# Dense products behind attention values issued as four 128x32 column tiles, with values directly after a score visit

## The chip, the cores and the metric

One NeuronCore of one Trainium2 chip runs the whole program. The metric is the device time of one execution in microseconds, a median over runs. "Span" is the profile's length of one execution; here it is 1.7 to 1.9 us shorter than the time. All runs told here are of the state that the records call fast, so fast runs are compared with fast runs throughout. (A fast run can still hold a few microseconds at a lower granted clock, as the kernel before does with 0.71 from 65 to 70 us; where one does, the text says so.) In these profiles every matmul has its weight load (10,928 of each in the kernel before); these two instructions per matmul are meant wherever "rows" are counted.

## The reference, cut to what matters

```python
def _A_ref(x, wqkv, wo):                 # S = 2048, D = 512, 32 heads of 16, window 256
    q, k, v = ...                        # x @ wqkv
    scores = einsum(q, k) * Dh ** -0.5   # masked to the last 256 positions
    o = einsum(softmax(scores), v)
    return o @ wo
def _B_ref(x, w_gate, w_up, w_down):     # F = 1792
    return (sigmoid(x @ w_gate) * (x @ w_up)) @ w_down
x = x + A(layernorm(x)); x = x + B(layernorm(x))      # twice
```

## The kernel before

The program is laid out by a scheduler written in Python. It keeps assumed times for every engine and transfer, and emits instructions in the order that its plan gives. What it assumes is never waited for by time: semaphores guard every access, so a wrong assumption costs waits, not results. TensorE's stream has three forms. Scores use four row tiles (32 rows by 128 columns), values four column tiles (128 by 32), and all dense products (q, k, v, output, gate, up, down) use the whole array. The scheduler fills the time between two score "visits" with dense products.

```python
def product_steps(...):                      # one of the dense kinds, cut
    return [(mm_ns(w), lambda kt=kt, o=o: nc.tensor.matmul(
        self.banks[bank][:, o:o + w], lhsT=self.wq[:, kt, ...], rhs=self.xnT[key][0][:, kt, o:o + w], ...))
        for o in range(0, TGW, w) for kt in range(KT)]

def values(...):                             # 16 groups of four and more, cut
    for k, (where, Va, p) in enumerate(parts):
        for g, h in enumerate(heads):        # four heads, four column tiles
            nc.tensor.matmul(o, lhsT=Va[:, c0:c0 + 32], rhs=p(h), ..., tile_position=(0, 32 * g))

def pick(self):                              # what TensorE does next, cut
    if pv and (wait <= 600 or wait > 1e8 or held):
        return self.do_values(pv, spare)     # values shortly before the next visit
    ...
    pl.count(1)
    end = pl.matmul("d", ns)                 # 96 ns are added in the plan where the form changes
```

The softmax here doesn't subtract the row's maximum and nothing guards it: scores larger than these inputs give would overflow.

## Time and profile before

| | kernel before |
|---|---|
| time, median of 3 | 556.89 us |
| span | 555.0 us |
| TensorE busy, share of span | 543.1 us, 98% |
| TensorE rows (2 x 10,928 in the profile; the prediction counts 21,858) | 21,856 |
| changes of form on TensorE | 380 |

A busy share hides what lies between two matmuls, because the recorded durations overlap: a values matmul of 64 columns is recorded with 193 ns in the mean, while the next group of four starts 0.03 us later. What sets the pace is the distance between starts, so the argument works with starts.

The busy times by stretch show where the kernel is fed worst. Columns are busy us and instructions per engine, then granted TensorE clock, DMA share and GB/s:

```profile
0.00:100.00 100.00, 93.75 (x1923) 65.69 (x1923) 74.39 (x181) 74.91 (x78) 20.19 (x53) 0.97 0.52 133
100.00:480.00 380.00, 378.64 (x8480) 244.15 (x8480) 299.41 (x641) 307.82 (x340) 43.51 (x88) 1.00 0.33 57
```

From 100 to 480 us TensorE, the first engine in the row, misses 1.4 us of 380. The list of what TensorE waited for (waiter, what ended the wait: us in total, times, longest) is short:

```profile
PE bank L529 <- DVE xn L517: 2.3, 2, 1.8
PE bank L929 <- issue: 1.9, 1, 1.9
PE bank L1104 <- POOL ident L438: 1.4, 1, 1.4
```

The first and last are the start of the program. The one in the middle, "issue", waited for nothing that the profile knows.

### The profile page before, as it was taken

The numbers are of one execution on the slowest core, as the hardware profiler recorded it, in microseconds if no ns is written. First come the engines' busy times: TensorE is split into PE (matmuls) and PEld (weight loads), VectorE is DVE, ScalarE is ACT, GpSimd is POOL, SyncE is SP. The second block draws the span as 40 slices with busy tenths as digits, with TensorE's granted clock in tenths as the row PEclk, the third lists the DMA queues.
The fourth block names the chain that finished last, engine by engine and source line by source line (L and its number), as shares of the span: only waits on it lengthen the run. The fifth ranks groups of instructions, "written<-read, shape, count | busy, mean of one in ns | idle before, by whom it ended". The sixth has DMA issues, their size and how long they took to land.

```text
span 555.0 us, 24233 instructions
## 1 busy us (share of the span) xinstructions
PE 543.1 (98%) x10928; PEld 361.3 (65%) x10928; DVE 406.4 (73%) x893; ACT 402.3 (72%) x468; POOL 65.3 (12%) x145
## 2 busy tenths in 40 slices
PE   7999899999999999999999999999999999999996
PEld 6567666665766656765566666566667666767873
DVE  5769787898976798688887778877777756464432
ACT  2869688888988878778788788787788876422321
POOL 5202111222010120002020010200010000010000
PEclk8999899999999999999999999999999999999999
DMA  8991203352323352424361303621133412310000
GB/s 276 290 216 33 41 18 67 46 85 44 70 34 47 59 90 47 64 43 79 50 95 29 58 12 69 89 51 41 31 70 80 68 32 51 69 48 11 11 20 28
DMA packets 99191, 36.94 MB, mean 67 GB/s; under 512 B 81424, under 2 KB 99088, under 8 KB 99088
## 3 DMA queue, kind: packets, MB, share of 16 engines
q1 hardware_dynamic: 97216, 33.56, 30.8%
q8 instruction: 85, 1.39, 1.1%
q10 hardware_dynamic: 1872, 1.84, 1.1%
q14 instruction: 18, 0.15, 0.1%
HBM read 9.70 MB, written 2.10 MB: 21 GB/s over the span
## 4 chain that ended last, share of the span: by engine, by line
PE 90%; DVE 5%; issue 1%; ACT 1%; POOL 1%; DMA 1%; SPq 0%; ACTq 0%; DVEq 0%
PE bank L659 34%; PE bank L692 18%; PE bank L929 8%; PE Sps L850 7%; PE bank L569 5%; PE bank L598 5%; PE bank L634 5%; PE bank L720 5%; PE Sps L860 2%; PE bank L1104 2%; DVE st L495 1%; DMA xnT<-xn 1%; DVE xn L517 1%; POOL st L501 1%; DVE PTring L788 0%
## 5 line engine op out<-in xcount | busy, mean ns | idle before, releaser
L902 ACT ACTIVATE PTring<-Sps 128x2048 bf16<-128x2048 f32 (+1 forms) x122 | 225.9, 1852 | 28.2 <-PE Sps L850 27.0
L659 PE MATMUL bank<-xnT,wg 128*128 128x256 bf16 (+1 forms) x1008 | 139.0, 262 | 0.8 <-ACT OTs L550 0.5
L659 PE MATMUL bank<-xnT,wu 128*128 128x256 bf16 (+1 forms) x1008 | 139.8, 262 | 0.0
L671 ACT ACTIVATE th<-bank 128x256 bf16<-128x256 f32 x224 | 80.3, 388 | 62.1 <-PE bank L659 59.1
L674 DVE SCALAR_TENSOR_TENSOR hT<-th,bank 128x256 bf16<-128x256 bf16 x224 | 87.2, 414 | 47.2 <-ACT th L671 46.6
L692 PE MATMUL bank<-wd,hT 128*128 128x512 bf16 x448 | 114.3, 381 | 0.0
L659 PEld LDWEIGHTS <-wg 128*128 128x128 bf16 x1008 | 88.4, 98 | 28.5 <-issue 3.6
L659 PEld LDWEIGHTS <-wu 128*128 128x128 bf16 x1008 | 90.0, 98 | 13.7 <-issue 1.6
L500 POOL TENSOR_SCALAR st<-st 128x1 f32<-128x1 f32 x64 | 20.6, 321 | 422.9 <-DVE st L496 422.9
L788 DVE TENSOR_TENSOR PTring<-PTring,mask 128x1024 bf16<-128x1024 bf16 x64 | 43.9, 686 | 31.0 <-ACT PTring L902 30.8
L902 ACT ACTIVATE edge<-Sps 128x2048 bf16<-128x2048 f32 (+1 forms) x32 | 56.7, 1771 | 12.9 <-PE Sps L860 12.9
L692 PEld LDWEIGHTS <-hT 128*128 128x128 bf16 x448 | 41.4, 98 | 37.4 <-issue 1.6
L929 PEld LDWEIGHTS <-Vaug 128*32 128x32 bf16 x2880 | 44.1, 97 | 15.0 <-issue 13.0
L929 PE MATMUL bank<-PTring,Vaug 128*32 128x64 bf16 (+1 forms) x2880 | 52.0, 203 | 1.9 <-issue 1.9
L850 PE MATMUL Sps<-qT,kTp 32*128 32x64 bf16 (+3 forms) x1856 | 48.5, 219 | 0.5 <-DVE st L495 0.2
L550 ACT CAST OTs<-bank 128x512 bf16<-128x512 f32 x40 | 29.4, 736 | 24.4 <-PE bank L929 23.7
L929 PE MATMUL bank<-edge,Vl 128*32 128x64 bf16 x1024 | 44.7, 193 | 0.0
L495 DVE BATCH_NORM_STATS2 st<-xsb 128x6 f32<-128x512 bf16 x64 | 43.7, 683 | 0.2
L850 PEld LDWEIGHTS <-kTp 32*128 32x128 bf16 x1856 | 24.9, 93 | 28.2 <-issue 24.5
L501 POOL TENSOR_TENSOR st<-st,nhalf 128x1 f32<-128x1 f32 x64 | 40.9, 640 | 5.3
L788 DVE TENSOR_TENSOR edge<-edge,maske 128x1024 bf16<-128x1024 bf16 x60 | 40.3, 679 | 0.8 <-ACT edge L902 0.7
L929 PE MATMUL bank<-edge,Vh 128*32 128x64 bf16 x896 | 40.7, 193 | 0.0
(71 smaller groups left out, 554.9 us busy)
## 6 DMA issues: line engine op xcount, KB each, us to landing
Vl<-Vaug SPq DMA_DIRECT2D x32, 68.0 KB, 2.9
out_dram<-xsb SPq DMA_DIRECT2D x32, 64.0 KB, 1.9
Vh<-Vaug SPq DMA_DIRECT2D x28, 68.0 KB, 2.2
wg<-in_B_w_gate_dram SPq DMA_DIRECT2D x2, 896.0 KB, 7.9
wu<-in_B_w_up_dram SPq DMA_DIRECT2D x2, 896.0 KB, 10.9
wd<-in_B_w_down_dram SPq DMA_DIRECT2D x7, 256.0 KB, 5.1
wq<-in_A_wqkv_dram ACTq DMA_DIRECT2D x3, 512.0 KB, 7.3
xsb<-in_A_x_dram SPq DMA_DIRECT2D x6, 256.0 KB, 6.2
```

The lines of the kernel that those rows point to most:

```text
L495: nc.vector.bn_stats(out=st[:, 0:6], in_=self.xsb[:, t, :])
L501: nc.gpsimd.tensor_tensor(out=st[:, 8:9], in0=st[:, 9:10], in1=self.nhalf[:], op=ALU.pow)
L550: self.nc.scalar.copy(out=out, in_=in_)
L569: return [(mm_ns(w), lambda kt=kt, o=o: nc.tensor.matmul(self.banks[bank][:, o:o + w], lhsT=self.wq[:, kt, cq * P:cq * P + P], rhs=self.xn ...
L659: return [(mm_ns(w), lambda i=i, j=j, fc=fc, wt=wt, kt=kt: nc.tensor.matmul(pt[:, i, j, :], lhsT=wt[:, kt, fc * P:(fc + 1) * P], rhs=self. ...
L671: nc.scalar.activation(out=box["th"][0][:], in_=pt[:, 0, :], func=AF.Tanh, scale=0.5)
L674: nc.vector.scalar_tensor_tensor(out=self.hT[:, chunk, :], in0=box["th"][0][:], scalar=1.0, in1=pt[:, 1, :], op0=ALU.add, op1=ALU.mult)
L692: nc.tensor.matmul(self.banks[bank][:], lhsT=self.hT[:, c, o:o + P], rhs=self.wd[:, fc, :], start=fc == 0, stop=fc == FC - 1)
L788: done = pl.task({"DVE": dve_bf_ns(1024)}, lambda e: nc.vector.tensor_tensor(out=r, in0=r, in1=m.to_broadcast([P, 16, HP]), op=ALU.mult), ...
L850: nc.tensor.matmul(self.sps[:, m, o:o + n * HP], lhsT=kTp[32 * m:32 * m + 32, i, tt, e, :], rhs=self.qT[32 * m:32 * m + 32, i, q0:q0 + n * ...
L902: nc.scalar.activation(out=out, in_=src, func=AF.Exp, scale=scale)
L929: nc.tensor.matmul(o, lhsT=Va[:, c0:c0 + 32], rhs=p(h), start=k == 0 or t == 0, stop=k == len(parts) - 1 or t == 0, tile_position=(0, 32 * g))
```

## The change

The intent is to save changes of form. Behind a values call TensorE is already in the 128x32 form, so dense products are issued in that form too, until the next score visit. Values are moved right behind a visit, which puts two needed changes (dense to scores, scores to values) where there were four. Around this core, priorities, weight loads (seven pieces instead of two), startup and the assumed DMA times were retuned.

```diff
+    def in_tiles(self):
+        return self.pl.mode == "pv" and self.slot < len(self.visits)
+    def product(self, out, lhsT, rhs, start, stop):
+        if not self.in_tiles():
+            self.nc.tensor.matmul(out, lhsT=lhsT, rhs=rhs, start=start, stop=stop)
+            return
+        for g in range(4):
+            h = slice(32 * g, 32 * g + 32)
+            self.nc.tensor.matmul(out[h], lhsT=lhsT[:, h], rhs=rhs, start=start, stop=stop, tile_position=(0, 32 * g))
 ...  (all dense nc.tensor.matmul calls become self.product)
-        if pv and (wait <= 600 or wait > 1e8 or held):
+        if pv and (pl.mode != "d" or wait <= -1 or wait > 1e8 or held):
-        pl.count(1)
-        end = pl.matmul("d", ns)
+        tiles = self.in_tiles() and u.name[0] != "tp"
+        pl.count(4 if tiles else 1)
+        end = pl.matmul("pv" if tiles else "d", ns + 0 if tiles else ns)
 ...  (retuning, the part that matters below)
-DMA_LATENCY = 1500
+DMA_LATENCY = 1200
-            self.dma_free = max(self.dma_free, self.now + ns) + nbytes / 250.0
+            self.dma_free = max(self.dma_free, self.now + ns) + nbytes / 290.0
-        b = pl.dma(1800, 262144, turn, ...)
+        b = pl.dma(1240, 160000, turn, ...)
-        d = pl.dma(1190, 131072, turn2, ...)
+        d = pl.dma(1190, 20000, turn2, ...)
-            d = pl.dma(1190, P * D * 2, ...)           # the third transpose
+            d = pl.dma(1210, 20000, ...)
 ...  (priorities, loads in seven pieces, startup: cut)
```

More of the change, by code (lines that the diff above doesn't have):

```diff
@@ L389, in load_x, with load @@
             return done
-        def load(dst, src, nbytes, after=0, deps=(), prio=2, queue="SP"):
+        def load(dst, src, nbytes, after=0, deps=(), prio=4, queue="SP"):
             ns = max(520, 40 + nbytes / 1024 * 0.95)
@@ L399, in loads @@
             h = slice("qkv".index(k) * D, ("qkv".index(k) + 1) * D)
-            self.has_wq[k] = load(self.wq[:, :, h], wq_src[:, :, h], D * D * 2, prio=0, queue="ACT" if i < 3 else "SP")
+            self.has_wq[k] = load(self.wq[:, :, h], wq_src[:, :, h], D * D * 2, prio=0, queue="ACT" if i < 2 else "SP")
         def x_group(g, after):
             h = slice(g * NBG, (g + 1) * NBG)
-            ev = load_x(self.xsb[:, h, :], h, NBG, 2 if g > 1 else 2, after=after)
+            ev = load_x(self.xsb[:, h, :], h, NBG, 4 if g > 1 else 2, after=after)
             for t in range(g * NBG, (g + 1) * NBG):
@@ L411, in loads @@
         at += gap * 2
-        n = F // 2
+        n = F // 7
         gu = []
-        for i in range(2):
+        for i in range(7):
             h = slice(i * n, (i + 1) * n)
@@ L418, in loads @@
                 pair.append(load(w[:, :, h], src[:, :, h], D * n * 2, after=at))
-                at += gap * 7 // 2
+                at += gap * 7 // 7
             gu.append(pair)
@@ L423, in loads @@
                 at += gap * 2
-        self.has_gu = [gu[fc * 2 // FC] for fc in range(FC)]
+        self.has_gu = [gu[fc * 7 // FC] for fc in range(FC)]
         self.has_wd = Event()
@@ L455, in constants @@
         self.pl.free["POOL"] = 4000.0
+        self.pl.free["SP"] = self.pl.free["ACT"] = 750.0
+        self.pl.at(750.0)
+        self.pl.at(1500.0)
         self.pl.free["DVE"] = 3200.0
@@ L524, in layer_norm @@
         o = (t % NBG) * P
-        if key == ("p", 0, 0) or key[0] == "g" and self.by_pe(key[1], t):
+        if key[:2] == ("p", 0) and t < 4 or key[0] == "g" and self.by_pe(key[1], t):
             def steps(bank):
@@ L534, in evac @@
                 d = pl.task({"ACT": act_ns(KT * P), "DVE": dve_ns(KT * P) + 100}, lambda e: self.copy(
-                    e, self.xnT[key][0][:, :, o:o + P], pt), [u.done], 0)
+                    e, self.xnT[key][0][:, :, o:o + P], pt), [u.done], 0 if t < NBG else 4)
                 d.done.then(lambda: (self.give(box["xn"]), done.fire()))
@@ L540, in layer_norm @@
         else:
-            d = pl.dma(1190, P * D * 2, lambda: nc.sync.dma_start_transpose(
+            d = pl.dma(1210, 20000, lambda: nc.sync.dma_start_transpose(
                 out=self.xnT[key][0][:, :, o:o + P], in_=box["xn"][0][:]), [c.done], prio)
@@ L568, in steps @@
         def steps(bank):
-            return [(mm_ns(w), lambda kt=kt, o=o: nc.tensor.matmul(
+            return [(mm_ns(w), lambda kt=kt, o=o: self.product(
                 self.banks[bank][:, o:o + w], lhsT=self.wq[:, kt, cq * P:cq * P + P], rhs=self.xnT[key][0][:, kt, o:o + w],
@@ L576, in evac @@
                 e, self.qT[:, cq, t0 * P:t0 * P + TGW].rearrange("p (t z k) -> p t z k", z=2, k=HP),
-                self.banks[u.bank][:].rearrange("p (t k z) -> p t z k", z=2, k=HP)), [u.done], 2)
+                self.banks[u.bank][:].rearrange("p (t k z) -> p t z k", z=2, k=HP)), [u.done], 3)
             d.done.then(self.q_ready[L, g, cq].fire)
@@ L597, in steps @@
         def steps(bank):
-            return [(mm_ns(w), lambda kt=kt, o=o: nc.tensor.matmul(
+            return [(mm_ns(w), lambda kt=kt, o=o: self.product(
                 self.banks[bank][:, o:o + w], lhsT=self.wq[:, kt, D + cq * P:D + cq * P + P], rhs=self.xnT[key][0][:, kt, o:o + w],
@@ L613, in split @@
                                             scalar1=self.rms[i][:, 0:1], scalar2=None, op0=ALU.mult)
-            a = pl.task({"ACT": act_ns(TGW), "DVE": dve_ns(TGW)}, cp, [u.done], 2, lambda: self.has("kt"))
-            b = pl.task({"DVE": 620}, split, [a.done], 2, port=True)
+            a = pl.task({"ACT": act_ns(TGW), "DVE": dve_ns(TGW)}, cp, [u.done], 3, lambda: self.has("kt"))
+            b = pl.task({"DVE": 620}, split, [a.done], 3, port=True)
             b.done.then(lambda: (self.give(box["kt"]), self.k_ready[L, g, cq].fire()))
@@ L633, in steps @@
         def steps(bank):
-            return [(mm_ns(D), lambda kt=kt: nc.tensor.matmul(
+            return [(mm_ns(D), lambda kt=kt: self.product(
                 self.banks[bank][:], lhsT=self.xnT[key][0][:, kt, o:o + P], rhs=self.wq[:, kt, 2 * D:3 * D],
@@ L641, in evac @@
             d = pl.task({"ACT": act_ns(D), "DVE": dve_ns(D)}, lambda e: self.copy(
-                e, dst, self.banks[u.bank][:].rearrange("p (i e c) -> p e i c", e=2, c=16)), [u.done], 2)
+                e, dst, self.banks[u.bank][:].rearrange("p (i e c) -> p e i c", e=2, c=16)), [u.done], 3)
             d.done.then(self.v_ready[L, t].fire)
@@ L658, in steps @@
             pt = self.banks[bank][:].rearrange("p (i f w) -> p i f w", i=2, w=w)
-            return [(mm_ns(w), lambda i=i, j=j, fc=fc, wt=wt, kt=kt: nc.tensor.matmul(
+            return [(mm_ns(w), lambda i=i, j=j, fc=fc, wt=wt, kt=kt: self.product(
                 pt[:, i, j, :], lhsT=wt[:, kt, fc * P:(fc + 1) * P], rhs=self.xnT[key][0][:, kt, c0:c0 + w],
@@ L675, in mult @@
                                                op0=ALU.add, op1=ALU.mult)
-            a = pl.task({"ACT": act_ns(GW)}, tanh, [u.done], 1, lambda: self.has("th"))
+            a = pl.task({"ACT": act_ns(GW)}, tanh, [u.done], 2, lambda: self.has("th"))
             b = pl.task({"DVE": dve_ns(GW)}, mult, [a.done], 1)
@@ L691, in mm @@
             c, o = (chunks[fc], (t - t0) * P) if n == 2 else (chunks[fc // 2], fc % 2 * P)
-            nc.tensor.matmul(self.banks[bank][:], lhsT=self.hT[:, c, o:o + P], rhs=self.wd[:, fc, :],
+            self.product(self.banks[bank][:], lhsT=self.hT[:, c, o:o + P], rhs=self.wd[:, fc, :],
                              start=fc == 0, stop=fc == FC - 1)
@@ L719, in steps @@
         def steps(bank):
-            return [(mm_ns(D), lambda c=c: nc.tensor.matmul(
+            return [(mm_ns(D), lambda c=c: self.product(
                 self.banks[bank][:], lhsT=b[0][:, c, :], rhs=self.wot[:, c, :],
@@ L727, in evac @@
                 out=self.xsb[:, t, :], in0=self.xsb[:, t, :], in1=self.banks[u.bank][:], op=ALU.add), [u.done], 1)
-            self.layer_norm(("g", L, t // NBG), t, [d.done], 0 if L * NT + t < 1 else 4)
+            self.layer_norm(("g", L, t // NBG), t, [d.done], 0 if L * NT + t < 2 else 3)
             return d.done
@@ L789, in job @@
                 out=r, in0=r, in1=m.to_broadcast([P, 16, HP]), op=ALU.mult), [x.done, self.has_mask],
-                {"m0": 2, "e0": 3, "e1": 6, "m2": 6}[what], port=True).done
+                {"m0": 2, "e0": 2, "e1": 6, "m2": 6}[what], port=True).done
             for hh in ((0, 1) if what[0] == "e" else (h,)):
@@ L937, in after_values @@
         box = self.outs.setdefault((L, t), {})
-        early = L * NT + t < 1
+        early = L * NT + t < 2
         def move(e):
@@ L956, in turn2 @@
             nc.sync.dma_start_transpose(out=b[0][:], in_=box["On"][0][:].rearrange("p c g x -> p (c g x)"))
-        a = pl.task({"DVE": dve_ns(512), "ACT": act_ns(512)}, move, [done], 0 if early else 1, lambda: "OTs" in box or self.has("OTs"))
+        a = pl.task({"DVE": dve_ns(512), "ACT": act_ns(512)}, move, [done], 0 if early else 2, lambda: "OTs" in box or self.has("OTs"))
         box[half] = a.done
@@ L965, in after_values @@
             return
-        b = pl.dma(1800, 262144, turn, [box[0], box[1]], 0 if early else 3)
+        b = pl.dma(1240, 160000, turn, [box[0], box[1]], 0 if early else 3)
         b.can = lambda: self.has("Oq")
@@ L970, in after_values @@
         c.done.then(lambda: (self.give(box["Oq"]), self.give(box["Rt"])))
-        d = pl.dma(1190, 131072, turn2, [c.done], 0 if early else 3)
+        d = pl.dma(1190, 20000, turn2, [c.done], 0 if early else 3)
         d.can = lambda: self.has("OnT")
@@ L1068, in pick @@
                 return self.do_values(pv, spare)
-            if spare and 1500 <= pl.now < 85000:
+            work = self.slot < len(self.visits) or self.open or self.oprojs or any(self.streams) or self.pv_list
+            if spare and work and 1500 <= pl.now < 85000:
                 self.keep_warm(min(spare, key=lambda i: self.bank_turn[i]))
@@ L1110, in pace @@
             return 0
-        if s < 0:
+        if s < 6:
             return 2500
@@ L1126, in copy @@
                 to, of = dst[e * HP:e * HP + HP, :, e * n:e * n + n], V[z:P:2, o:o + 2, e * n:e * n + n]
-                parts.append(pl.dma(580, HP * n * 4, lambda to=to, of=of: nc.sync.dma_start(out=to, in_=of), deps, 3).done)
+                parts.append(pl.dma(580, HP * n * 4, lambda to=to, of=of: nc.sync.dma_start(out=to, in_=of), deps, 4).done)
             when_all(parts, done.fire)
@@ L1177, in choose @@
                     continue
-                if u.ready() and self.can_go(u) and not (u.on_act and busy_act >= 4):
+                if u.ready() and self.can_go(u) and not (u.on_act and busy_act >= 3):
                     cand.append((self.rank(u), 1, u))
```

## The prediction

> **What bounds the kernel now.** I read the page first, then the totals of stretches, then TensorE's timeline in steady state, then the chain of waits around the one long gap. The page:
>
> ```profile
> PE 543.1 (98%) x10928; PEld 361.3 (65%) x10928; DVE 406.4 (73%) x893; ACT 402.3 (72%) x468; POOL 65.3 (12%) x145
> PE   7999899999999999999999999999999999999996
> PEclk8999899999999999999999999999999999999999
> q8 instruction: 85, 1.39, 1.1%
> PE 90%; DVE 5%; issue 1%; ACT 1%; POOL 1%; DMA 1%; SPq 0%; ACTq 0%; DVEq 0%
> ```
>
> The reader is to see that TensorE is the bound throughout: 98% busy, 90% of the chain that ended last, and no slice after the first that falls back. VectorE and ScalarE, at 73% and 72%, follow. So the question is only what TensorE's own stream costs. "Busy" hides two things, though: matmuls overlap, and their modelled ends cover the pauses between them. So I went from busy times to starts. Steady state, around a values burst:
>
> ```profile
> 237.72 1.24 PE L692 MATMUL bank<-wd,hT 128*128 128x512 bf16 x5
> 238.89 0.27 PE L929 MATMUL bank<-PTring,Vaug 128*32 128x128 bf16 x8
> 238.98 0.20 PE L929 MATMUL bank<-edge,Vh 128*32 128x64 bf16 x4
> 239.01 0.20 PE L929 MATMUL bank<-PTring,Vaug 128*32 128x64 bf16 x4
> 239.04 0.20 PE L929 MATMUL bank<-edge,Vl 128*32 128x64 bf16 x4
> ...
> 240.25 0.21 PE L929 MATMUL bank<-edge,Vl 128*32 128x64 bf16 x4
> 240.40 0.40 PE L850 MATMUL Sps<-qT,kTp 32*128 32x256 bf16 x8
> 240.73 1.47 PE L692 MATMUL bank<-wd,hT 128*128 128x512 bf16 x6
> ```
>
> First, a group of four 64-wide column-tile matmuls (128*32), with its four weight loads, starts every 0.03 us: four tiles together take what one full matmul of that width takes. Second, wherever the form changes (128*128, 128*32, 32*128) there is a pause: from 240.25 plus 0.03 to 240.40, and from 240.40 plus 2 x 0.109 to 240.73, is about 0.11 us each. Over the whole trace, start to start less the streaming time of the last group, the six kinds of change have medians of 93 to 109 ns. There are 380 changes, about 38 us.
>
> So the span splits up. Streaming at the measured 56, 109 and 216 ns per 128-, 256- and 512-wide product: dense 417.3 us (11.2 of it warm-up on the identity), values 41.4, scores 33.8; changes 38; sum 530.5. Of 555.0, 24.5 us are left: about 8.4 in the first 20 us, 4.6 after its last matmul, a few short waits, and this, in the middle of a values burst:
>
> ```profile
> 61.31 0.20 PE L929 MATMUL bank<-PTring,Vaug 128*32 128x64 bf16 x3
> 63.38 0.19 PE L929 MATMUL bank<-PTring,Vaug 128*32 128x64 bf16 x1 [1.86 <-issue]
> ```
>
> Three of a group of four run, then nothing for 2.03 us (start to start, less streaming), and no engine is named. No semaphore can stand there. The stretches after it show a second price:
>
> ```profile
> 60.00:65.00 5.00, 3.14 (x134) 1.85 (x122) 3.02 (x7) 3.06 (x3) 0.64 (x2) 0.95 0.03 8
> 65.00:70.00 5.00, 5.00 (x79) 4.02 (x79) 3.27 (x7) 2.98 (x4) 0.00 (x0) 0.71 0.30 52
> ```
>
> The granted clock falls to 0.71. Ten microseconds there hold 3.6 us of loss in all, 2.0 of gap and some 1.6 of slow clock.
>
> [...]four 32-column loads and four matmuls fit in 0.03 us. [...]1.39 MB in 85 packets is 16.4 KB each, and 21,858 TensorE rows in the build over 256 is 85.4.[...]
>
> **The change, part by part.** I compared the instruction orders of the two builds.
>
> 1. Changes of form: 380 before, 321 after. Changes between dense and values fall from 72 to 13, those between dense and scores from 256 to 197, and those between scores and values rise from 52 to 111. 59 x 0.1 us = 5.9 us saved, all on TensorE, so on the path.
>
> 2. Dense in column tiles: 756 of the 3,000 dense products become 3,024 matmuls. By the 0.03 us groups each product streams in the same time: 0.
>
> 3. Warm-up matmuls: 200 to 148. 52 x 56 ns = 2.9 us, if real work takes their place. Gate and up weights in seven pieces allow that: the first gate product stands at 34.8 us of streaming instead of 38.5. The weights take about 9.4 MB at the 220 to 290 GB/s of the first slices, so landings before some 38 us are not obviously late. I count 2.9 us.
>
> 4. Reordered priorities and the limit on gate/up banks move VectorE and ScalarE work that is off the path: 0, plus or minus 2 us.
>
> Sum of the intended effects: 521.7 us of stream instead of 530.5, 8.8 us less.
>
> 5. Instructions: TensorE rows go from 21,858 to 26,290, +4,432, or 103 blocks instead of 85. They come in the wrong place. A values call is 160 instructions in 0.68 us; before, dense followed at two instructions per product. Now eight per product follow: 256-wide, 8 in 109 ns, or 73 per us; 128-wide, 143 per us. A block of 256 can be used up in 1.6 to 3 us.
>
> What can the fetch sustain? One packet took 1.1% x 16 x 555 / 85 = 1.15 us. The gap above falls at row 2,240, which fits a block boundary (9 x 256 less 64 rows); its fetch started at 60.68 us, landed at 61.87, and TensorE resumed at 63.38. The block before, worth 1.56 us of streaming, lasted 3.65 us from its first matmul to the next block's first. Two other blocks of 3.03 and 3.01 us lasted 3.35 and 3.29; blocks of 3.44 and 3.50 lost under 0.03. So a block needs about 3.3 to 3.7 us[...], and less after slow dense work[...]: an estimate from these rows.
>
> I then summed the streaming time of each block. Shortfall against 2.7, 3.0 and 3.3 us: before, 1.1, 1.4 and 2.5 us in 1, 1 and 4 blocks. After, 10.6, 18.0 and 26.4 us in 18, 26 and 29 blocks, and shifting the boundaries changes this by only a few us. [...]I choose 17 us, against about 2.6 in the kernel before: +14.4 us. Short gaps of about 0.7 us may lower the clock here and there: +1.
>
> 6. Sum: 555.0 - 8.8 + 14.4 + 1 = 561.6 us of span; times run 1.9 us above the span (556.89 against 555.0): 563.5. I take 1.5 off[...]: 562.
>
> **The rivals.** Hidden fetch: the 61 us gap is a single accident, and 128-wide and 256-wide tile streams don't outrun the fetch. For it: 84 of 85 boundaries show at most some 0.3 us[...]. Against it: the gap is at the boundary, and bursts this dense were rare before. Then 8.8 us go, the 2.6 and 1.6 of that gap too: 544 to 547 us. Full starvation: every tile run pays 3.6 us per block[...]: +24 us instead of +14, and the clock falls more often: 570 to 576. Late weights: the order in the first 60 us now trusts earlier landings; if they are late, TensorE waits in place of warming up, 2 to 4 us back. Slow tile weight loads: 98 ns per load not hidden would show in the values bursts, where it doesn't; unlikely.
>
> **Range and chances.** Mine is most likely, 555 to 571. The hidden-fetch rival has one chance in four and straddles the 2% line (545.8). The upper line is 568.0, inside the upper half of my own estimate. Range 546 to 573; faster 0.14, same 0.56, slower 0.30.
>
> **What would show each step.** Right: 321 changes of about 0.1 us; 756 products in tiles, four starts together every 56, 109 or 216 ns; about 103 instruction packets on q8; some twenty gaps on TensorE of 0.3 to 2 us with "issue" as releaser, inside values bursts or the tile products after them, 256 rows apart or a multiple of it; "issue" growing to some 4% of the chain. Wrong: no such gaps, and a span near 543 us, means that the fetch keeps up and step 5 falls; tile products that start further apart than full ones mean that step 2 falls; gaps whose releaser is a DMA or ScalarE mean that the reordering (4) was not free.

## The result, and the profile after

| | before | after |
|---|---|---|
| time, median | 556.76 us (4 runs) | 578.08 us (4 runs, 575.7 to 580.13) |
| span of the profiled run | 555.0 us | 574.0 us |
| TensorE busy | 543.1 us (98%) | 539.6 us (94%) |
| changes of form | 380 | 321 |

The ratio is 1.0384, with a 95% interval of 1.0335 to 1.0432. Here and below a ratio is the mean time of one kernel's fast runs over that of the other's in the same rounds, so not quite the ratio of the medians quoted. The change is slower by 3.8%.

The page of the changed kernel, the rows that answer to those of the prediction:

```profile
PE 539.6 (94%) x13144; PEld 360.9 (63%) x13144; DVE 421.4 (73%) x911; ACT 392.7 (68%) x450; POOL 62.7 (11%) x145
PE   7999897999998999989999999999989999999997
PEclk8999999999999999999999999999999999999999
q8 instruction: 102, 1.67, 1.3%
PE 79%; DVE 7%; DMA 6%; issue 5%; ACT 2%; POOL 0%; SPq 0%; ACTq 0%
```

TensorE is busy for less time in a longer span, at the same clock (0.995 granted in the mean, 0.994 before), and the chain that ended last now has 5% "issue" and 6% DMA in it, where each had 1%. The middle stretch shows that the loss is spread through the steady state:

```profile
0.00:100.00 100.00, 88.28 (x2329) 60.66 (x2333) 76.14 (x183) 70.70 (x73) 19.68 (x53) 0.98 0.59 133
100.00:480.00 380.00, 362.16 (x9872) 235.79 (x9873) 302.48 (x635) 294.22 (x313) 40.12 (x86) 1.00 0.32 56
```

TensorE now misses 17.8 us of those 380, against 1.4. What it waited for:

```profile
PE bank L570 <- issue: 11.8, 10, 2.1
PE Sps L866 <- issue: 2.9, 3, 1.0
PE bank L945 <- issue: 2.5, 3, 1.9
PE bank L532 <- DVE xn L520: 2.0, 1, 2.0
...
PE bank L566 <- issue: 1.4, 2, 1.1
PE bank L566 <- DMA xnT<-xn: 1.3, 3, 0.6
PE Sps L876 <- issue: 1.1, 2, 0.8
PE bank L566 <- DMA OnT<-On: 1.0, 2, 0.6
PE bank L945 <- DMA Vl<-Vaug: 1.0, 2, 0.7
PE bank L570 <- DMA OnT<-On: 1.0, 1, 1.0
```

"Issue" is 19.7 us in 20 waits (11.8 + 2.9 + 2.5 + 1.4 + 1.1), where it was 1.9 in one. L570 are the new tile products, L945 values, L866 and L876 scores. Waits for DMA landings are 4.3 us, where they were 0.5. One of the waits, in TensorE's timeline:

```profile
70.21 0.20 PE L945 MATMUL bank<-edge,Vl 128*32 128x64 bf16 x4
70.24 0.56 PE L570 MATMUL bank<-xnT,wg 128*32 128x128 bf16 x26
72.38 0.29 PE L570 MATMUL bank<-xnT,wg 128*32 128x128 bf16 x6 [1.59 <-issue]
72.46 0.66 PE L570 MATMUL bank<-xnT,wu 128*32 128x128 bf16 x32
```

The gap splits a single accumulation over 32 matmuls, after the 26th, in the middle of a group of four tiles: nothing that the program waits for can stand there. Right after it, 32 matmuls of 128 columns take 0.44 us (72.46 to 72.90), which is eight products at 55 to 56 ns; whole products of 128 columns start 56 ns apart at the median in the same trace. So the tile form itself streams at the rate of whole products.

Measured from start to start less the streaming time, 25 such gaps add up to 24.4 us. (I leave out eight more that stand at a unit's start or repeat such a gap, where a transfer explains them.) Each comes where TensorE's row count crosses a multiple of 256 less an offset that drifts from 64 to 86: rows 2496, 2752, 3008, 4032, 4538, and so on. In the DMA records one instruction packet, of 16,384 bytes, belongs to each. From the first matmul of the block before to its fetch passed 1.05 us (median), the packet took 1.11, and from landing to TensorE's next matmul it was 1.37 us (1.2 to 1.7 in all 25). That makes 3.6 us per block of 256 rows at the median, but from 2.4 to 4.5 us among the 25: how early the fetch started differs, from 0.0 to 2.0 us after that first matmul (timed for 23 of them). Where the block's own work is shorter than that, TensorE stands. The packets themselves took no longer than the 1.15 us that the prediction worked out for the kernel before, so the fetch did not get slower; more blocks came too fast for it.

The sum then closes: 555.0 - 8.8 (stream and changes, as counted in the prediction) + 21.8 (gaps at block boundaries, 24.4 instead of 2.6) + 6.0 (what is left over, of which the list of waits gives 3.8 as waits for landings) = 574.0 us.

### The profile page after: what moved, and what is told of

Read it like the earlier page. It is cut to its first block, busy times and chain, and to the rows that moved or that the text cites. A ratio compares the mean times of both kernels' runs of the same rounds, so it can differ in the third digit from the quotient of the medians.

```text
span 574.0 us, 28647 instructions
## 1 busy us (share of the span) xinstructions
PE 539.6 (94%) x13144; PEld 360.9 (63%) x13144; DVE 421.4 (73%) x911; ACT 392.7 (68%) x450; POOL 62.7 (11%) x145
## 4 chain that ended last, share of the span: by engine, by line
PE 79%; DVE 7%; DMA 6%; issue 5%; ACT 2%; POOL 0%; SPq 0%; ACTq 0%
PE bank L566 46%; PE bank L570 16%; PE bank L945 8%; PE Sps L866 6%; DMA OnT<-On 3%; DMA Oq<-OTs 2%; PE Sps L876 2%; ACT PTring L918 1%; DVE st L498 1%; DMA xnT<-xn 1%; DVE PTring L804 1%; DVE xn L520 1%; DMA Vl<-Vaug 1%; PE bank L1122 1%; ACT edge L918 1%
## 5 line engine op out<-in xcount | busy, mean ns | idle before, releaser
L690 DVE SCALAR_TENSOR_TENSOR hT<-th,bank 128x256 bf16<-128x256 bf16 x224 | 88.2, 414 | 45.0 <-ACT th L687 44.6
L566 PE MATMUL bank<-xnT,wu 128*128 128x256 bf16 (+1 forms) x765 | 107.0, 263 | 0.3 <-issue 0.3
L566 PE MATMUL bank<-xnT,wg 128*128 128x256 bf16 (+1 forms) x732 | 101.9, 262 | 1.7 <-DMA xnT<-xn 1.1
L566 PE MATMUL bank<-wd,hT 128*128 128x512 bf16 x388 | 98.3, 380 | 0.0
L566 PEld LDWEIGHTS <-wg 128*128 128x128 bf16 x732 | 64.6, 98 | 23.7 <-issue 3.4
L566 PEld LDWEIGHTS <-wu 128*128 128x128 bf16 x765 | 68.8, 98 | 10.9 <-issue 1.6
L503 POOL TENSOR_SCALAR st<-st 128x1 f32<-128x1 f32 x64 | 18.5, 289 | 435.7 <-DVE st L499 433.9
L566 PEld LDWEIGHTS <-hT 128*128 128x128 bf16 x388 | 36.2, 98 | 31.5 <-issue 0.8
L945 PE MATMUL bank<-PTring,Vaug 128*32 128x64 bf16 (+1 forms) x2880 | 53.2, 203 | 2.2 <-issue 2.1
L866 PE MATMUL Sps<-qT,kTp 32*128 32x64 bf16 (+3 forms) x1856 | 48.9, 218 | 3.8 <-issue 2.9
L555 DVE CAST OTs<-bank 128x512 bf16<-128x512 f32 x57 | 42.2, 741 | 13.7 <-PE bank L945 12.8
L945 PEld LDWEIGHTS <-Vaug 128*32 128x32 bf16 x2880 | 44.7, 97 | 11.5 <-issue 8.0
L570 PE MATMUL bank<-xnT,wg 128*32 128x256 bf16 (+1 forms) x1104 | 41.3, 258 | 10.3 <-issue 10.2
L866 PEld LDWEIGHTS <-kTp 32*128 32x128 bf16 x1856 | 25.2, 92 | 39.9 <-issue 37.1
L945 PE MATMUL bank<-edge,Vl 128*32 128x64 bf16 x1024 | 45.1, 193 | 1.4 <-DMA Vl<-Vaug 1.0
L566 PE MATMUL bank<-xnT,wq 128*128 128x512 bf16 (+1 forms) x193 | 42.8, 360 | 0.0
```

The lines of the kernel that those rows point to most:

```text
L503: nc.gpsimd.tensor_scalar(out=st[:, 9:10], in0=st[:, 7:8], scalar1=1e-5, scalar2=None, op0=ALU.add)
L555: self.nc.vector.tensor_copy(out=out, in_=in_)
L566: self.nc.tensor.matmul(out, lhsT=lhsT, rhs=rhs, start=start, stop=stop)
L570: self.nc.tensor.matmul(out[h], lhsT=lhsT[:, h], rhs=rhs, start=start, stop=stop, tile_position=(0, 32 * g))
L690: nc.vector.scalar_tensor_tensor(out=self.hT[:, chunk, :], in0=box["th"][0][:], scalar=1.0, in1=pt[:, 1, :], op0=ALU.add, op1=ALU.mult)
L866: nc.tensor.matmul(self.sps[:, m, o:o + n * HP], lhsT=kTp[32 * m:32 * m + 32, i, tt, e, :], rhs=self.qT[32 * m:32 * m + 32, i, q0:q0 + n * ...
```

## The experiments

Three theories. Fetch: the tile form makes eight instructions of two, and behind a values call they outrun the fetch of instructions. Order: the new order of values, with its trust in early landings, makes TensorE wait. Form: column tiles stream slower by themselves. The kernel before was run beside all of them; its medians were 555.55 to 556.19 us.

### e1: the same order, products whole

```diff
-        if not self.in_tiles():
+        if True:
```

The plan still counts four, so nothing moves; only the instructions are fewer.

> The order of all work is exactly that of the changed kernel; only the 756 products in tiles are issued whole again, so 21,752 TensorE rows instead of 26,290, and 377 changes of form instead of 321. Fetch theory: the 26 us of gaps at block boundaries fall to some 2 to 4 us, the changes cost 5.6 us more, so the span falls from 574 to about 556 (time 555 to 560). Rival, that the new order and its trust in early landings is what costs: the gaps stay, time 572 or more. Rival, that column-tile products stream slower than whole ones: also a drop, but the product spacing of the changed kernel (109 and 216 ns) speaks against it already.

Measured: 558.57 us, inside the range, ratio to the kernel before 1.0052 (1.0018 to 1.0086). The list of waits has no "issue" left:

```profile
PE bank L566 <- DMA OnT<-On: 4.2, 4, 1.6
PE bank L532 <- DVE xn L520: 2.1, 1, 2.1
PE bank L566 <- DMA xnT<-xn: 1.7, 2, 1.5
PE bank L1122 <- POOL ident L438: 1.4, 1, 1.4
PE bank L945 <- DMA Vl<-Vaug: 1.3, 2, 1.1
```

So 19.5 of the 21.3 us go with the tile form alone (578.08 - 558.57), although 56 changes of form come back. What stays is 7.2 us of waits for landings, more than in the changed kernel.

### e2: the two named parts on the kernel before, without the retuning

```diff
 # the kernel before, with in_tiles, product, the new rule in pick and the tile count as in the change; nothing else
```

> The kernel before with only the two named parts: the tile form behind values, and values directly after a visit; all priorities, loads and assumed DMA times as before. 25,626 rows, 631 products in tiles, 325 changes. Fetch theory: some 22 us of gaps at block boundaries, less 5.5 us of changes: time 567 to 575. Rival, that the retuning around it is to blame: 551 to 557.

Measured: 586.27 us, ratio 1.0535 (1.0503 to 1.0566), 11 us above the top of what I expected. "Issue" is 18.4 us in 16 waits, as the theory has it. The rest is new: TensorE's waits for ScalarE make 6.2 us in all, and from 100 to 160 us the granted clock is 0.90, which is some 6 us by my estimate (a tenth of 60 us). Why both come in this order of work isn't shown. So the core is what costs. With the retuning, but the assumed DMA times of the kernel before, the same core took 575.12 us (e5 below), so the new priorities and loads won some 11 us of it back.

### e3: the retuning alone

```diff
-        if pv and (pl.mode != "d" or wait <= -1 or wait > 1e8 or held):
+        if pv and (wait <= 600 or wait > 1e8 or held):
-        tiles = self.in_tiles() and u.name[0] != "tp"
+        tiles = False
```

> The changed kernel with whole products and the old rule for values, so only the retuned priorities, loads and assumed DMA times. 21,696 rows, 380 changes, 120 warm-up matmuls. Fetch theory: 2 to 4 us at block boundaries; span 550 plus up to 6 us of waits for landings: time 551 to 559. Rival, that the retuning is to blame: above 565.

Measured: 568.88 us, ratio 1.0225 (1.0202 to 1.0247): a miss for the fetch theory: 10 us above its range, and over the 565 us that stood for the rival. Only 2.6 us are "issue". DMA waits are 6.7 us, ScalarE 4.7. So a second cause exists beside the fetch; e5 and e8 to e10 look for it.

### e4: the same work, shifted by half a block

```diff
+        for i in range(64):
+            self.nc.tensor.matmul(self.banks[BANKS - 1][:, 0:8], lhsT=self.ident[:], rhs=self.ident[:, 0:8], start=True, stop=True)
         pl.run(self.pick)
```

> The changed kernel with 128 TensorE rows (64 matmuls of 8 columns) added at the very start, where TensorE waits for its first input. Fetch theory: the gaps come at the same rows modulo 256 of the new count (170 to 192), so at other work: near new rows 1726, 2238, 2750, 3262, 4286 and 4798 with 0.9 to 1.9 us each, and not at the old work of rows 2496, 3008, 4032 and 4538 (new 2624, 3136, 4160, 4666); about the same sum, 20 to 28 us, and the time within 1% of the changed kernel's. Rival, that the gaps come from what the instructions at those places wait for: they stay with the old work.

Measured: 582.94 us (two runs), 0.8% above the changed kernel. "Issue" is 21.2 us in the list of waits, against 19.7. The rows, in each kernel's own count:

| changed kernel | shifted by 128 rows | where it would be if it stayed with its work |
|---|---|---|
| 2496: 1.42 us | 2242: 1.71 us | 2624: none |
| 3008: 1.76 us | 2752: 2.14 us | 3136: none |
| 4032: 1.87 us | 3264: 1.70 us | 4160: none |
| 4538: 2.32 us | 4288: 1.44 us | 4666: none |

There are also gaps at 1726 (0.61 us) and 4794 (1.52 us): all six places that I had named, two of them outside the sizes that I had given (0.61 and 2.14 us, for 0.9 to 1.9). One of them, in the shifted kernel, stands in scores, whose instructions the change didn't touch:

```profile
75.36 0.34 PE L570 MATMUL bank<-xnT,wg 128*32 128x128 bf16 x12
75.64 0.40 PE L866 MATMUL Sps<-qT,kTp 32*128 32x64 bf16 x14
77.44 0.26 PE L866 MATMUL Sps<-qT,kTp 32*128 32x192 bf16 x2 [1.40 <-issue]
```

The gap follows the count of instructions, not the work. That settles the cause of the 24.4 us: neither what the work at those places waits for nor the tile form by itself can explain gaps that move with the count.

### e5: the changed kernel with the assumed DMA times of the kernel before

```diff
-DMA_LATENCY = 1200
+DMA_LATENCY = 1500
-... nbytes / 290.0
+... nbytes / 250.0
 (and the three transposes' times and sizes as before the change)
```

> The changed kernel with the five assumed DMA times of the kernel before, tile form kept (782 products, 26,492 rows, 322 changes). Fetch theory: my sums of blocks give 22 us of gaps at block boundaries; if the waits for landings (9 us outside the boundaries in the changed kernel, 3 in the one before) come from too early an assumption, they fall to 3 to 5: time 566 to 573. Rival, that those waits come from the fetches themselves, which hold up the landings: they stay, time 573 to 580.

Measured: 575.12 us, ratio 1.0335 (1.0303 to 1.0367), 3 us less than the changed kernel and 2 above my range, a miss. The two intervals overlap (1.0335 to 1.0432 for the changed kernel), so the 3 us in time aren't clear of the noise. In the traces, waits for landings are 1.3 us instead of 4.3, so the rival that fetches hold the landings up falls. "Issue" is listed at 22.6 us in 44 waits, but this trace lacks 76 matmul records (13,170 matmuls to 13,246 weight loads), which look like small waits; so its sum isn't used.

### e6 and e7: fewer products in tiles

```diff
 # e6: only 512-wide products
+        self.wide = ns > 200
-        return self.pl.mode == "pv" and self.slot < len(self.visits)
+        return self.pl.mode == "pv" and self.slot < len(self.visits) and self.wide
 # e7: only where the block that is being read would last 3.7 us (entered: when the plan entered it)
+        self.fits = pl.now + (256 - (pl.issued + 70) % 256) / 8 * ns >= pl.entered + 3700
```

> The changed kernel, but only the 512-wide products behind values go in tiles: 8 instructions in 216 ns, half the density of the 256-wide. 212 products in tiles, 23,016 rows, 361 changes. Fetch theory: 5 us of gaps at boundaries instead of 26: time 557 to 563. Rival, that the tile form costs by itself, per product: 212 of 756 products keep 28% of the loss over whole products, 19.5 us, which would also be 564; the sum of the gaps tells them apart.

> The changed kernel, but a product behind values goes in tiles only where the block of 256 rows that is being read, used up at the tile rate, would still last 3.7 us from its start. 250 products in tiles, 23,244 rows, 356 changes. Fetch theory: about 2 us of gaps at boundaries, stream and changes 525.0 us against 527.3 with whole products: time 553 to 560, level with e1 or up to 2.5 us under it. Rival: as for e6, a third of the loss, 564 to 566.

Measured: e6 569.67 us, ratio 1.0246; e7 564.55 us, ratio 1.015 (1.0102 to 1.0199). Both times are misses, 4 to 7 us over my ranges. The gaps did what was expected: 6.3 us of "issue" in e6, leaving out 19 entries of at most 0.2 us where records are missing, and 0.4 us in values in e7, with none in a tile product. The time of e7 by itself is where the rival put it (564 to 566), so it is the gaps, and e8 below, that speak against the rival. Other waits grew. In e7, whose profile is of the slowest of its four runs (568.28 us), these are

```profile
PE bank L568 <- DMA xnT<-xn: 5.7, 6, 1.3
PE bank L568 <- DMA OnT<-On: 3.9, 5, 2.1
PE bank L568 <- issue: 3.6, 22, 0.2
PE bank L947 <- DVE PTring L806: 3.2, 3, 1.7
```

(The 3.6 us of "issue" are 22 entries of at most 0.2 us: missing records, 82 in this trace.) With the fetch gaps gone, TensorE arrives earlier than the transposes land, and waits for them instead. That points to a second cause, which e8 and e10 test: the plan of the changed kernel places work before its data can be there. The changed kernel's plan gives a transpose of OTs 3.0 us from issue to landing and one of OnT 2.5 us (worked out from its issue time, bytes, rate and `DMA_LATENCY`, with no transfer ahead of it), where the kernel before gave 4.3 and 3.2. The medians in the changed kernel's trace are 3.3 and 2.5 us, so about half of the landings come later than the plan says.

### e8: the fetch-aware kernel with the old assumed DMA times

> The same with the assumed DMA times of the kernel before: 231 products in tiles, 23,146 rows, 359 changes, 3.6 us of gaps by my sums; waits for landings back to about 3 us: time 551 to 557, faster than the kernel before by up to 1%, if landings are what is left; level with e7 if they are not.

Measured: 556.37 us, ratio 0.9997 (0.9967 to 1.0026), inside the range. Against e7, whose only difference is the assumed times, 8.2 us are gone, with 231 products still in tiles; so the tile form doesn't cost by itself. DMA waits are 4.3 us instead of 10.9.

### e9 and e10: the old assumed DMA times without tiles

> e1 (no tiles, values directly after a visit) with the assumed DMA times of the kernel before: 21,800 rows, 379 changes, stream and changes 528.8 us. If too early an assumption made the 7 us of waits for landings in e1, they fall to 1 to 3 us: time 552 to 557. If they belong to the order of values, they stay: 558 to 561.

> e3 (retuning alone) with the assumed DMA times of the kernel before. e3 took 568.9 us where its stream is shorter than that of the kernel before. If the assumed landings are the cause: 552 to 558. If the priorities are: 562 or more.

Measured: e10 555.41 us, ratio 1.0005 (0.9979 to 1.0031), where e3 took 568.88. So the early assumptions made e3 slow, and in this order of values the other retuned priorities and loads cost nothing. e9 is a miss: 560.88 us, ratio 1.0085 (1.0056 to 1.0115), against 558.57 of e1, although its DMA waits fell from 7.2 to 3.3 us. Its profiled run was its fastest (557.93), and in it two gaps of 2.7 us together came at "issue". What made its other runs slower I can't say from that trace. So the early assumption isn't what e1 loses: from e1 to e9 no gain shows (-2.3 us, with overlapping intervals). Going back to the old assumed times gave 13.5 us in e3, 8.2 in e7, 3.0 in the changed kernel (not clear of the noise) and nothing in e1; why it depends so much on the order stays open. And e9 against e10, in the same rounds, shows that the new order (values directly after a visit, planned as for tiles but with whole products) costs 5.5 us by itself here: it isn't free either. The traces kept don't show why.

### e11 and e12: the margin of the fetch-aware kernel

```diff
 # e8 with other margins
-        ... >= pl.entered + 3700
+        ... >= pl.entered + 4200      # e11;  3300 in e12
```

> e8 with a wider margin, 4.2 us of a block instead of 3.7: 110 products in tiles, 22,420 rows, 372 changes, 527.0 us of stream and changes, 0.5 us of gaps at boundaries by my sums. Fetch theory: 551 to 556, at or just under the kernel before; the saving of form changes left is only 0.8 us.

> e8 with a narrower margin, 3.3 us: 365 products in tiles, 23,950 rows, 353 changes, 525.1 us of stream and changes, 3.8 us of gaps at boundaries. Fetch theory: what the form changes save over e11, 1.9 us, is given back as gaps, 3.3 us: 553 to 559, 0 to 3 us over e11.

Both fell in their ranges. Measured: e11 554.70 us, ratio 0.9989 (0.9966 to 1.0013), with 0.8 us of "issue" in two waits; e12 557.58 us, ratio 1.004 (1.0017 to 1.0063), with 6.0 us in seven. On e11's page, the queue of instruction fetches (packets, MB, share of the 16 DMA engines) and the shares of the chain that ended last are

```profile
q8 instruction: 87, 1.43, 1.1%
PE 90%; DMA 4%; DVE 3%; ACT 1%; issue 1%; ACTq 0%
```

Fetches are back from 102 to 87, and "issue" on the chain from 5% to 1%, close to the kernel before (85 and 1%). More products in tiles save changes of form and lose more in gaps. The best version found is level with the kernel before, not faster.

## Why the prediction was right or wrong

The prediction said 562 us, in a range up to 573; measured were 578.08. Two terms of its sum failed. Step 5, the fetch, had the right mechanism, shown by e1 and e4, and the wrong size: 24.4 us instead of 17. Step 4 had the path wrong: it put the retuning off the critical path, at 0 plus or minus 2 us, and priced only reordered work of VectorE and ScalarE. What it left out, the earlier landing times that the plan assumes, is on the path: TensorE's waits for landings grew by 3.8 us, part of 6.0 us outside the other terms.

- Step 1, changes of form: right. 321 were found, with a median of about 100 ns.
- Step 2, products in tiles stream as fast as whole ones: right. Their starts lie 56, 109 and 216 ns apart at the median, as those of whole products do.
- Step 3, warm-up: right as far as the traces show. The 52 matmuls are gone, and the first gate product starts at 44.6 us instead of 47.3, 2.7 us earlier. The rival "late weights" falls: TensorE's list has no wait for the gate, up or down weights. (The 9.4 MB in that step must include the input: the loads of weights alone come to 7.6 MB.)
- Step 4, the retuning, put at 0 plus or minus 2 us: wrong. Everything outside stream, changes and boundaries grew by 6.0 us, of which the list of waits gives 3.8 to DMA landings. e3 against e10 (13.5 us) and e7 against e8 (8.2 us) show that the assumed times can cost that much and more. In the changed kernel itself e5 takes 3.0 us off both the waits and the time, the latter not clear of the noise; the 2.2 us beside the landings stay unexplained.
- Step 5, the fetch, put at 17 us against 2.6: this is the term that was mis-sized. It measured 24.4. My own sum of blocks gave 18.0 at 3.0 us per block and 26.4 at 3.3, so 24.4 is what some 3.2 us per block gives; I then chose 9 us less, for a block that needs less after slow dense work, and that was too much. The 9 us were my estimate. The trace of the kernel before does show early fetches where work is slow: for its last four packets, behind blocks of 14 to 17 us, the fetch started 0.6 to 1.9 us before the first matmul of the block before. But at the gaps it started 0.0 to 2.0 us after it, and no run tests what sets this. The stalled blocks needed 2.4 to 4.5 us, so no single time per block is exact.
- The lowered clock, put at 1 us: didn't show. The granted clock was 0.995 against 0.994 before, and none of the 25 gaps, of up to 2.3 us, was followed by a slow stretch. In e4 the slice of the page that holds the gap ending at 68.4 us (57.9 to 72.3 us) has clock digit 8 (80 to 90%), where the slices beside it have 9. So the 0.71 after the one gap of the old profile is no rule.
- Slips that changed little: the page has a slice after the first that falls back (the fifth shows 8, which is the gap at 61 us), 256 rows of 256-wide tile products last 3.5 us and not 3, and the 1.9 us between span and time are of different runs (the profiled run's own time was 556.7, so 1.7).

With 7.4 us more in step 5, 6.0 in step 4 and 1.0 less for the clock, the 561.6 us of span worked out in the prediction become 574.0. The 1.5 us taken off at the end were in the wrong direction, and the profiled run was the fastest of the four, 2.4 us under their median.

Of the rivals, "hidden fetch" fell with e1 and e4; "slow tile weight loads" fell with the spacing. "Full starvation" was given 570 to 576, which the profiled run met (575.7) and the median did not. It came near partly by luck: its +24 us for the fetch is close to the measured +21.8, but the slower clock that it added didn't come, and the 6.0 us of step 4 took its place. The chance of 0.30 for slower was too low for a loss that three blocks of the old profile already showed (they lasted 3.65, 3.35 and 3.29 us for 1.56, 3.03 and 3.01 us of streaming).

## What to carry to other kernels

A form that saves time on the array (here 59 changes of about 0.1 us) can cost it at the instruction stream (here 24.4 us of gaps). Count instructions per block of 256, one packet of 16,384 bytes in these traces, and hold the time of each block against what stalled blocks needed in your profile (here 3.6 us at the median, 2.4 to 4.5 in all); do it for every block, not for the mean. A margin of 4.2 us left 0.8 us of gaps (e11), one of 3.3 us left 6.0 (e12). When a wait is taken out of a static plan, check the assumed landing times again against the landings of the new trace: in e7, with the fetch gaps out of the tile products, TensorE waited 10.9 us for landings, and 4.3 us with the later times of e8.
